# A decode step with gated attention and MLP: another layout and place for the last output weights, and a repeated TensorE block with its values behind its scores

## The chip, the cores and the metric

The kernel runs on one core of a Trainium2 chip. The metric is device time in microseconds from the start to the end of one execution; a run's time is that of its only core. Engines are named as the profile names them: PE (TensorE; PEld are its weight loads), DVE (VectorE), ACT (ScalarE), POOL (GpSimd) and SP (SyncE, which issues nearly all loads). All tensors are float32.

## The reference, cut to what matters

One token goes through an attention block over a cache of 32,768 positions and through a gated MLP, and a scalar gate mixes the two:

```python
g = _sigmoid((x * gate_w).sum(-1, keepdims=True))
q = x @ wq                                      # 32 heads of 128, D = 512
scores = einsum("bhqd,bhkd->bhqk", q, k) * Dh ** -0.5   # 8 kv heads, 4 query heads each
p = softmax(scores)
a = einsum("bhqk,bhkd->bhqd", p, v).reshape(1, 1, 4096) @ wo
b = (silu(x @ w1) * (x @ w3)) @ w2              # F = 1792
out = g * a + (1 - g) * b
```

The two caches hold 128 MB each, so nearly all of the time goes into reading them.

## The kernel before

**Tiles and buffers.** Two kv heads make a pair w, 0 to 3. The keys of a pair are read in four rounds of 8 MB, so there are 16 rounds t, 0 to 15. The values of one kv head h are read in two parts of 8 MB, v0 to v15 with number s = 2h + e. The buffer `big_a` (regions A0 and A1 of 4 MB) takes keys, `big_b` (B0 and B1) values, apart from the start, where `big_b` takes keys too. `wo_t` holds the 2 MB of wo that belong to one pair; wo0 to wo3 below are these four parts, one after the other in the same buffer.

**A round** (L453 to L476). DVE transposes the keys in 32x32 blocks, eight instructions (`scores`); PE multiplies each with the queries, laid out by ACT in `winc`; ACT copies the scores from PSUM to `sb` (`scores_out`) and PE clears the bank with a product of zeros (L244). At the end of a pair `turn` transposes the scores on PE into `turned`, and `softmax` (L378) takes the maximum and the exponentials, with DVE before and behind ACT; it leaves the probabilities in `prob` and their sums in `sums`. `weights` copies those that a value part needs to `pv`, `values_loop` multiplies them with the part on PE (64 matmul records), and `own` folds the result on DVE. Values lag behind keys by LAG = 5 rounds: PE takes v(t-5) at the head of round t.

**Order.** `Program` records every operation and derives semaphores from names of what is read and written. Each engine works strictly in the order of recording: an instruction that waits holds up everything behind it on its engine, and on SP a load that waits for its buffer holds up the loads behind it. PE's part of the 16 rounds is a hardware loop (L674 to L689), written out a second time; inside it a branch on the round's number skips values in the first rounds. Waits on other engines use counters that PE takes down (`take`).

**The end** (L568 to L655). v12 to v15 are loaded half by half: v12 and v14 through A0 and A1, v13 and v15 through `big_b`, v15 in four pieces of 4, 2, 1 and 1 MB (pieces 0 to 3; L596 to L599). v11, whose weights were made in the loop, is multiplied behind it (L579). `norm` sums `sums` over partitions and takes the reciprocal times the gate, `heads` makes the output of each head (`on`), `place` (L511) turns two pairs' outputs or one's into a row layout (`own_rows`), in which partition p holds the values of rows 8p to 8p + 7 of that pair's wo, by a DVE product, a PE product with `spot`, a DVE product with `mask` and a DVE sum. `mix_pair` then adds eight rows of wo per partition into `acc`, with eight instructions on DVE (L532). wo3 comes in another layout, one row per partition and tile (L488), so that head 6 can be mixed from `on` with four instructions on DVE and head 7 be multiplied on PE from `otp` without `place`.

**The tail.** w2 is loaded in five parts over A0 (L608). `last_head` (L555) folds the values of a head with four DVE instructions, multiplies on PE and scales into its destination. Then PE multiplies head 7's output with four tiles of wo3 (L634), DVE mixes four rows of w2 into `acc` (L635), PE takes four more rows of w2 (L637), DVE adds both (L638), and `ff_down` (L649) brings `acc` and the last six rows of w2 together; the result is copied and sent out. `idle_product` (L612) is a product whose result nobody reads; five stand between the last steps.

Of the kernel before, what the change touches and what calls it, by code (L numbers as in the profile page):

```python
# [116 lines left out]
def kernel(  # L117
# [27 lines left out]
    R = NB * DH  # L145
    NP = HKV // 2
    NH = 4 * NP
    LAG = 5
    FR = F // P
    FJ = F // 4  # L150
    assert DH == P and D == 4 * P and REP == 4 and HKV == 8 and F == FR * P and S == 4 * P * NB
# [9 lines left out]
    def sbuf(name, *shape):  # L161
        return nc.alloc_sbuf_tensor(name, [P, *shape], F32)[:]
# [12 lines left out]
    silu = tmp[:, 0].rearrange("p b d -> p (b d)")  # L175
    red = [sbuf(f"red{h}", P) for h in range(6)]
    acc = sbuf("acc", 512)
    otp = sbuf("otp", REP, 32)
    htp = sbuf("htp", FR, 32)
    turned = nc.alloc_psum_tensor("turned", [P, 2048], F32)[:]  # L180
    pf = [turned[:, 512 * f:512 * f + 512] for f in range(4)]
# [149 lines left out]
    def load_keys(t):  # L331
        b = where(t)
        for z in range(2):
            load(region(b, z), kd[t // 4, t % 4, z], ["AB"[b] + str(z)])
# [15 lines left out]
    def scores(t, z, win_op):  # L350
        kin = region(where(t), z).rearrange("p (n c j) -> p c n j", c=4, j=32)
        key = "AB"[where(t)] + str(z)
        for c in range(4):
            dst = kt[c % 2].rearrange("p (n i) -> p n i", i=32)
            k = dve(lambda c=c, d=dst: V.transpose(d, kin[:, c]), reads=[key], writes=[f"kt{c % 2}"], credit="keys")  # L355
            pe(lambda c=c: scores_part(c), reads=[f"kt{c % 2}", "winc"], writes=["s"], loop=True,
               credits=((win_op, 1), (k, 1)) if c == 0 else ((k, 1),))
# [75 lines left out]
                    )  # L433
        return ins

    def values_loop(vt, wt, loop=True):
        pe(values_all, reads=["B0", "B1", "pv", "pvpad"], writes=["o"], credits=((vt, 16), (wt, 1)), loop=loop)


    def own(s):  # L440
        h, e = divmod(s, 2)
        dve(lambda: V.tensor_tensor(
            tmp[:, e], ps_o.rearrange("p (b d) -> p b d", b=4), own_b.unsqueeze(2).to_broadcast([P, 4, P]), op=ALU.mult,
        ), reads=["o", "own_b"], writes=[f"tmp{e}"])
        if e == 1:
            dve(lambda: V.tensor_reduce(red[h], tmp.rearrange("p e b d -> p d (e b)"), axis=AX.X, op=ALU.add),  # L446
                reads=["tmp0", "tmp1"], writes=[("red", h)])
# [3 lines left out]
    vals = {}  # L451
    first = window(0, 0)
    for t in range(NH):  # L453
        scores(t, 0, first)
        second = window(t, 1)
        if t >= LAG:
            own(t - LAG)
            vals[t - LAG + 1] = (vals[t - LAG + 1], weights(t - LAG + 1))
        scores(t, 1, second)
        scores_out(t)  # L460
        if t + 1 < NH:
            load_keys(t + 1)
        if t % 4 == 3:
            turn()
        if t + 1 < NH:
            first = window(t + 1, 0)

        if t in (4, 7, 11, 15):
            softmax(t // 4 if t > 4 else 0)
        if t == LAG - 1:  # L470
            vals[0] = (vals[0], weights(0))
        if t + 1 < NH:
            if t >= LAG - 1:
                values_loop(*vals.pop(t - LAG + 1))
            if t >= LAG - 2:
                vals[t - LAG + 2] = load_values(t - LAG + 2)  # L476


    own_rows = sbuf("own_rows", 3, 8)
    each = [sbuf(f"each{i}", 2, 8, 8) for i in range(2)]  # L480

    def load_wo(w):
        src = wo[w * 8 * P:(w + 1) * 8 * P, :]
        if w < NP - 1:

            load(wo_t, src.rearrange("(p k) e -> p k e", k=8), ["wo"])
        else:
            load(wo_t, src.rearrange("(t p) e -> p t e", p=P), ["wo"])  # L488


    def norm(ws):
# [16 lines left out]
            reads=["m1"] + [("recip", h // 2) for h in hs], writes=[("on", h) for h in hs])  # L508


    def place(ws):  # L511
        i, n, w0 = ws[0] % 2, len(ws), ws[0]
        mine = each[i][:, 0:n]
        dve(lambda: V.tensor_mul(  # L514
            mine, on[:, 8 * w0:8 * w0 + 8 * n].rearrange("p (w t) -> p w t", w=n).unsqueeze(2).to_broadcast([P, n, 8, 8]),
            own_k.unsqueeze(1).unsqueeze(3).to_broadcast([P, n, 8, 8]),
        ), reads=["own_k"] + [("on", 2 * w + u) for w in ws for u in range(2)], writes=[f"each{i}"])
        pe(lambda: T.matmul(  # L518
            pm[i][:, 0:64 * n], spot.rearrange("p t x -> p (t x)"), mine.rearrange("p w k t -> p (w k t)"),
            start=True, stop=True,  # L520
        ), reads=["spot", f"each{i}"], writes=[f"m{i}"])
        dve(lambda: V.tensor_mul(
            mine, pm[i][:, 0:64 * n].rearrange("p (w k t) -> p w k t", w=n, t=8),
            mask.unsqueeze(1).unsqueeze(1).to_broadcast([P, n, 8, 8]),
        ), reads=[f"m{i}", "mask"], writes=[f"each{i}"])
        dve(lambda: V.tensor_reduce(own_rows[:, w0:w0 + n], mine, axis=AX.X, op=ALU.add),
            reads=[f"each{i}"], writes=[("own", w) for w in ws])


    def mix(o, key, ks, t=None, tkey="wo"):  # L530
        for k in ks:
            dve(lambda k=k: V.scalar_tensor_tensor(  # L532
                acc, (wo_t if t is None else t)[:, k, :], o(k), acc, op0=ALU.mult, op1=ALU.add,
            ), reads=[tkey, key, "acc"], writes=["acc"])

    def mix_pair(w):
        mix(lambda k: own_rows[:, w, k:k + 1], ("own", w), range(8))


    def values(h, e, z, vt, key, groups=range(4)):  # L540
# [14 lines left out]
    def last_head(h):  # L555
        r = red[h % 2]
        dve(lambda: V.tensor_scalar(r, ps_o[:, 0:P], own_b[:, 0:1], None, op0=ALU.mult),  # L557
            reads=["o", "own_b"], writes=[("red", h % 2)])
        for b in range(1, 4):
            dve(lambda b=b: V.scalar_tensor_tensor(  # L560
                r, ps_o[:, b * P:(b + 1) * P], own_b[:, b:b + 1], r, op0=ALU.mult, op1=ALU.add,
            ), reads=["o", "own_b", ("red", h % 2)], writes=[("red", h % 2)])
        pe(lambda: T.matmul(pm[1][:, 0:REP], r, own_q, start=True, stop=True), reads=["own_q", ("red", h % 2)], writes=["m1"])
        dst = on[:, 24:28] if h == 6 else otp[:, :, 0]
        dve(lambda: V.tensor_mul(dst, pm[1][:, 0:REP], recip[:, 4 * h:4 * h + 4]),
            reads=["m1", ("recip", 3), "otp"], writes=[("on", h)])

    def load_halves(s):  # L568
        for z in range(2):
            load(region(0, z), vd[s // 2, s % 2][:, z * R:z * R + R], [f"A{z}"])  # L570

    load_wo(0)
    load_halves(12)
    norm(range(3))
    heads(range(5))
    place((0, 1))
    mix_pair(0)
    load_wo(1)
    values_loop(*vals.pop(11), loop=False)  # L579
    load(big[1], vd[6, 1], ["B0", "B1"])  # L580
    own(11)
    norm(range(3, 4))
    heads(range(5, 6))
    mix_pair(1)
    load_wo(2)
    for z in range(2):
        values(6, 0, z, region(0, z), f"A{z}")
    load_halves(14)
    load_wo_late = lambda: load_wo(3)
    place((2,))  # L590
    mix_pair(2)
    load_wo_late()
    for z in range(2):
        values(6, 1, z, region(1, z), f"B{z}")
    last_head(6)
    cuts = (0, R, R + 4096, R + 6144, 2 * R)  # L596
    names = ("B0", "B1a", "B1b", "B1c")
    for (a, b), n in zip(zip(cuts, cuts[1:]), names):
        load(big[1][:, a:b], vd[7, 1][:, a:b], [n], over=[] if n == "B0" else ["B1"])  # L599
    mix(lambda k: on[:, 24 + k:25 + k], ("on", 6), range(4))  # L600
    for z in range(2):
        values(7, 0, z, region(0, z), f"A{z}")

# [17 lines left out]
    idle_product(512)  # L621
    idle_product(256)
    last_head(7)
    pa, pb = pf[0], pf[1]

    def ff_wide(ks, w, t, **kw):
        def go():
            for k in ks:
                j = k % 4
                ins = T.matmul(pa[32 * j:32 * j + 32, :], w(k), t(k), start=(k < 4), stop=(k >= 4))  # L630
            return ins
        pe(go, writes=["f0"], **kw)

    ff_wide(range(4), lambda k: otp[:, k, :], lambda k: wo_t[:, 4 + k, :], reads=[("on", 7), "otp", "wo"])  # L634
    mix(lambda k: htp[:, k, 0:1], "htp", range(4), w2t, ("w2", 0))  # L635
    idle_product(256)
    ff_wide(range(4, 8), lambda k: htp[:, k, :], lambda k: w2t[:, k, :], reads=["htp", ("w2", 4)])  # L637
    dve(lambda: V.tensor_add(acc, acc, pa), reads=["acc", "f0"], writes=["acc"])  # L638
    idle_product(512)

# [32 lines left out]

    with nc.Fori(0, NP, 1, engines=[PE], head_slot={PE: 0}):  # L674
        with nc.Fori(0, 4, 1, engines=[PE]):
            with T.If_cmp(half, LAG, "IS_GE"):
                take("values", 16)
                take("weights")
                values_all().then_inc(done, 1)
            with nc.Fori(0, 2, 1, engines=[PE]):  # L680
                take("windows")
                for c in range(4):
                    take("keys")
                    scores_part(c).then_inc(done, 1)
            take("scores")
            zeros().then_inc(done, 1)
            T.reg_add(half, half, 1)
        for f in range(4):
            turn_part(f).then_inc(done, 1)  # L689
# [31 lines left out]
```

## Time and profile before

| | |
|---|---|
| three runs | 697.03, 696.72, 696.99 us; median 696.99 |
| the profiled execution | 696.78 us, of which 694.8 us span |
| busy in the span | PE 405.1 us (58%), DVE 382.6 (55%), ACT 45.3 (7%), POOL 2.5 |
| mean granted TensorE clock | 0.767 |
| read from HBM | 296.23 MB, 426 GB/s over the span |

Times in all views count from the start of the span. In a timeline each line gives start, duration, engine and line, operation, what is written and read, the number of instructions taken together, and in brackets the engine's idle time before it with what ended that. The granted clock is the share of TensorE's clock pulses that the hardware let through; in this kernel it is 0.50 or 1.00 at any moment. A load's entry gives its size and the time from issue to landing; loads of one queue land in the order of their issue. A matmul in float32 shows as two records.

### The profile page before, as it was taken

Reading aid. Unit: us, or ns where it says so; the run is one execution under the profiler, and the core shown is the slowest. Engines: PE = TensorE matmul, PEld = TensorE weight load, DVE = VectorE, ACT = ScalarE, POOL = GpSimd, SP = SyncE. Lnnn points to the kernel's source line nnn. Section 1 sums busy time; section 2 is a strip of 40 time slices with the busy share of each in tenths; the row PEclk is TensorE's granted clock in tenths of the full one; section 3 lists DMA queues with packets and bytes.
Section 4 is the critical chain, followed back from the end, with each engine's and each line's share of the span. In section 5 each row is a group of like instructions: output and inputs, shape, how many; then the busy total and the mean of one; then the engine's idle time right before and its main releaser. Section 6 shows DMA issues by size and latency. Waiting matters only on the chain. (4 is left out here: it accounts for less than half of the span.)

```text
span 694.8 us, 5662 instructions
## 1 busy us (share of the span) xinstructions
PE 405.1 (58%) x2386; PEld 93.6 (13%) x2386; DVE 382.6 (55%) x274; ACT 45.3 (7%) x90; POOL 2.5 (0%) x15
## 2 busy tenths in 40 slices
PE   3626566656656656647565665647556563655447
PEld 1100011201110102101010102101010102211112
DVE  1029988796619085854629095844529095732113
ACT  0200000011100001000100001000100001000000
POOL 1000000000000000000000000000000000000000
PEclk9976888897676776867778879877886766666759
DMA  9999999999999999999999999999999999999996
GB/s 383 425 429 438 436 423 440 459 398 436 445 417 455 419 449 413 443 417 443 453 402 451 423 430 431 460 402 447 430 421 451 421 451 407 426 444 424 409 427 285
DMA packets 10421, 296.36 MB, mean 427 GB/s; under 512 B 1062, under 2 KB 1066, under 8 KB 2476
## 3 DMA queue, kind: packets, MB, share of 16 engines
q1 hardware_dynamic: 10402, 296.23, 99.2%
q8 instruction: 6, 0.10, 0.1%
q14 instruction: 3, 0.02, 0.0%
q10 hardware_dynamic: 10, 0.00, 0.0%
HBM read 296.23 MB, written 0.00 MB: 426 GB/s over the span
## 5 line engine op out<-in xcount | busy, mean ns | idle before, releaser
L355 DVE STREAM_TRANSPOSE kt<-big_a 128x2048 f32<-128x2048 f32 x112 | 250.1, 2286 | 171.1 <-DMA big_a<-in_A_k_cache_dram 165.5
L344 PE MATMUL ps<-kt,winc 128*32 128x512 f32 x1024 | 189.8, 824 | 134.4 <-PEq L671 134.4
L430 PE MATMUL ps<-big_b,pv 128*32 128x512 f32 x768 | 110.7, 741 | 59.6 <-PEq L671 59.6
L344 PEld LDWEIGHTS ps<-kt,winc 128*32 128x32 f32 x1024 | 27.1, 124 | 290.8 <-issue 290.8
L430 PEld LDWEIGHTS ps<-big_b,pv 128*32 128x32 f32 x768 | 30.0, 133 | 139.1 <-issue 139.1
L355 DVE STREAM_TRANSPOSE kt<-big_b 128x2048 f32<-128x2048 f32 x16 | 35.7, 2285 | 4.1 <-PE ps L344 2.1
L244 PE MATMUL ps<-acc 128*128 128x512 f32 x34 | 24.3, 805 | 21.8 <-PEq L671 20.3
L548 PE MATMUL ps<-big_b,probs 128*32 128x512 f32 x128 | 19.5, 771 | 22.2 <-DMA big_b<-in_A_v_cache_dram 22.2
L338 ACT COPY winc<-win 128x128 f32<-128x128 f32 x32 | 9.8, 306 | 328.0 <-PE ps L344 328.0
L532 DVE SCALAR_TENSOR_TENSOR acc<-wo_t,own_rows,acc 128x512 f32<-128x512 f32 x24 | 18.0, 752 | 23.4 <-DMA wo_t<-in_A_wo_dram 22.6
L361 ACT COPY sb<-ps 128x512 f32<-128x512 f32 x16 | 17.0, 1063 | 154.4 <-PE ps L344 154.4
L548 PE MATMUL ps<-big_a,probs 128*32 128x512 f32 x128 | 20.7, 812 | 5.8 <-DMA big_a<-in_A_v_cache_dram 5.8
L403 DVE TENSOR_REDUCE sums<-probs 128x8 f32<-128x2048 f32 x4 | 15.6, 3890 | 8.0 <-ACT probs L398 8.0
L381 DVE TENSOR_REDUCE mt<-turned 128x8 f32<-128x2048 f32 x4 | 9.1, 2282 | 17.8 <-PE turned L371 17.8
L270 PE MATMUL turned<-big_a,xp 128*32 128x512 f32 x64 | 11.9, 913 | 2.6 <-DMA big_a<-in_A_wq_dram 2.3
L307 PE MATMUL turned<-big_b,xp 128*32 128x448 f32 x64 | 7.7, 632 | 9.4 <-DMA big_b<-in_B_w_dram 9.4
L532 DVE SCALAR_TENSOR_TENSOR acc<-wo_t,on,acc 128x512 f32<-128x512 f32 x4 | 3.0, 752 | 16.4 <-DMA wo_t<-in_A_wo_dram 16.3
L244 PEld LDWEIGHTS ps<-acc 128*128 128x128 f32 x34 | 6.3, 231 | 42.2 <-issue 40.7
L446 DVE TENSOR_REDUCE red<-tmp 128x128 f32<-128x1024 f32 x6 | 11.5, 1913 | 0.2
L557 DVE TENSOR_SCALAR red<-ps,own_b 128x128 f32<-128x128 f32 x2 | 0.7, 348 | 17.8 <-PE ps L548 17.8
L518 PE MATMUL ps<-each,spot 128*128 128x128 f32 (+1 forms) x4 | 1.2, 400 | 15.0 <-DVE each L514 15.0
L398 ACT ACTIVATE probs<-turned 128x1024 f32<-128x1024 f32 x8 | 7.8, 1021 | 32.9 <-DVE turned L393 32.9
(82 smaller groups left out, 111.4 us busy)
## 6 DMA issues: line engine op xcount, KB each, us to landing
big_a<-in_A_k_cache_dram SPq DMA_DIRECT2D x28, 4096.0 KB, 28.0
big_b<-in_A_k_cache_dram SPq DMA_DIRECT2D x4, 4096.0 KB, 31.5
big_a<-in_A_v_cache_dram SPq DMA_DIRECT2D x4, 4096.0 KB, 32.6
big_a<-in_A_wq_dram SPq DMA_DIRECT2D x2, 4096.0 KB, 16.5
wo_t<-in_A_wo_dram SPq DMA_DIRECT2D x4, 2048.0 KB, 17.9
big_b<-in_B_w_dram SPq DMA_DIRECT2D x2, 3584.0 KB, 33.7
big_b<-in_A_v_cache_dram SPq DMA_DIRECT2D x1, 4096.0 KB, 27.8
big_b<-in_A_v_cache_dram SPq DMA_DIRECT2D x1, 2048.0 KB, 23.1
```

Of the source, the lines that this page charges most:

```text
L244: return T.matmul(ps_s, acc[:, 0:P], acc, start=True, stop=False, skip_group_check=True)
L270: ins = T.matmul(pf[b][32 * j:32 * j + 32, :], xp[:, c, :], t[:, o:o + REP * DH], start=(c == 0), stop=(c == NC - 1),)
L338: lambda: A.copy(winc, win[:, t // 4, :, 16 - 16 * z:48 - 16 * z]),
L344: ins = T.matmul(ps_s[32 * g:32 * g + 32, :], winc[:, c, :], kt[c % 2][:, 512 * g:512 * g + 512], start=False, stop=False, skip_group_chec ...
L355: k = dve(lambda c=c, d=dst: V.transpose(d, kin[:, c]), reads=[key], writes=[f"kt{c % 2}"], credit="keys")
L361: lambda: A.copy(sb[:, :, :, t % 4], ps_s.rearrange("p (n i) -> p n i", i=32)),
L381: dve(lambda: V.tensor_reduce(mt[:, 0:8], turned.rearrange("p (n q) -> p q n", q=8), axis=AX.X, op=ALU.max), reads=banks, writes=["mt"])
L403: dve(lambda: V.tensor_reduce(sums[:, 8 * w:8 * w + 8].rearrange("p (u q) -> p u q", u=2), probs[:, :, 0:1024].rearrange("p u (n q) -> p u ...
L430: ins = T.matmul(ps_o[32 * t:32 * t + 32, :], pv[:, o:o + 32], big[1][:, n * P:(n + 4) * P], start=((z, g) == (0, 0)), stop=((z, g) == (1, ...
L446: dve(lambda: V.tensor_reduce(red[h], tmp.rearrange("p e b d -> p d (e b)"), axis=AX.X, op=ALU.add), reads=["tmp0", "tmp1"], writes=[("red ...
L532: dve(lambda k=k: V.scalar_tensor_tensor(acc, (wo_t if t is None else t)[:, k, :], o(k), acc, op0=ALU.mult, op1=ALU.add,), reads=[tkey, ke ...
L548: ins = T.matmul(ps_o[32 * t:32 * t + 32, :], prob[u][:, o:o + 32], vt[:, n * P:(n + 4) * P], start=((e, z, g) == (0, 0, 0)), stop=((e, z, ...
```

## The change

LAG becomes 4, and PE takes v(t-4) behind the scores of round t instead of v(t-5) ahead of them; so v11 is part of the loop, ahead of the last `turn`. A softmax now stands in the round in which its first values are taken: softmax 0 stays in round 4, 1 and 2 move from rounds 7 and 11 to 8 and 12, and 3 moves from round 15 to behind the loop, after `own(11)`. All four parts of wo come in one layout, eight rows to a partition. `place` handles pairs 0 to 2 in one pass, and pair 3 in a second one behind `last_head(7)`, which writes to `otp`, now eight wide. The loads are in another order: v12, wo0, v13, wo1, v14, wo2, pieces 0 and 1 of v15, wo3, pieces 2 and 3, w2; before it was wo0, v12, wo1, v13, wo2, v14, wo3, the four pieces, w2. In the tail PE takes four rows of w2 first, then eight of wo3 (both heads of the pair), then four of w2, into one bank, and the four mixes of w2 on DVE and the four of head 6 are gone.

```diff
     NH = 4 * NP
-    LAG = 5
+    LAG = 4
     FR = F // P
...
-    otp = sbuf("otp", REP, 32)
+    otp = sbuf("otp", 8, 32)
...
-    def values_loop(vt, wt, loop=True):
-        pe(values_all, reads=["B0", "B1", "pv", "pvpad"], writes=["o"], credits=((vt, 16), (wt, 1)), loop=loop)
+    def values_loop(vt, wt):
+        pe(values_all, reads=["B0", "B1", "pv", "pvpad"], writes=["o"], credits=((vt, 16), (wt, 1)), loop=True)
...
     first = window(0, 0)
     for t in range(NH):
+        v = t - LAG
         scores(t, 0, first)
         second = window(t, 1)
-        if t >= LAG:
-            own(t - LAG)
-            vals[t - LAG + 1] = (vals[t - LAG + 1], weights(t - LAG + 1))
+        if v >= 1:
+            own(v - 1)
+            if v % 4:
+                vals[v] = (vals[v], weights(v))
         scores(t, 1, second)
         scores_out(t)
         if t + 1 < NH:
             load_keys(t + 1)
+            first = window(t + 1, 0)
+
+        if v >= 0 and v % 4 == 0:
+            softmax(v // 4)
+            vals[v] = (vals[v], weights(v))
+        if v >= 0:
+            values_loop(*vals.pop(v))
+        if v + 1 >= 0 and t + 1 < NH:
+            vals[v + 1] = load_values(v + 1)
         if t % 4 == 3:
             turn()
-        if t + 1 < NH:
-            first = window(t + 1, 0)
-
-        if t in (4, 7, 11, 15):
-            softmax(t // 4 if t > 4 else 0)
-        if t == LAG - 1:
-            vals[0] = (vals[0], weights(0))
-        if t + 1 < NH:
-            if t >= LAG - 1:
-                values_loop(*vals.pop(t - LAG + 1))
-            if t >= LAG - 2:
-                vals[t - LAG + 2] = load_values(t - LAG + 2)
 
     own_rows = sbuf("own_rows", 3, 8)
-    each = [sbuf(f"each{i}", 2, 8, 8) for i in range(2)]
...
     def load_wo(w):
-        src = wo[w * 8 * P:(w + 1) * 8 * P, :]
-        if w < NP - 1:
-
-            load(wo_t, src.rearrange("(p k) e -> p k e", k=8), ["wo"])
-        else:
-            load(wo_t, src.rearrange("(t p) e -> p t e", p=P), ["wo"])
+        load(wo_t, wo[w * 8 * P:(w + 1) * 8 * P, :].rearrange("(p k) e -> p k e", k=8), ["wo"])
...
-    def place(ws):
-        i, n, w0 = ws[0] % 2, len(ws), ws[0]
+    def place(ws, rows, i, over=()):
+        n, w0 = len(ws), ws[0]
...
-        dve(lambda: V.tensor_reduce(own_rows[:, w0:w0 + n], mine, axis=AX.X, op=ALU.add),
-            reads=[f"each{i}"], writes=[("own", w) for w in ws])
-
-
-    def mix(o, key, ks, t=None, tkey="wo"):
-        for k in ks:
+        dve(lambda: V.tensor_reduce(rows, mine, axis=AX.X, op=ALU.add),
+            reads=[f"each{i}", *over], writes=[("own", w) for w in ws])
+
+
+    def mix(w):
+        for k in range(8):
             dve(lambda k=k: V.scalar_tensor_tensor(
-                acc, (wo_t if t is None else t)[:, k, :], o(k), acc, op0=ALU.mult, op1=ALU.add,
-            ), reads=[tkey, key, "acc"], writes=["acc"])
-
-    def mix_pair(w):
-        mix(lambda k: own_rows[:, w, k:k + 1], ("own", w), range(8))
+                acc, wo_t[:, k, :], own_rows[:, w, k:k + 1], acc, op0=ALU.mult, op1=ALU.add,
+            ), reads=["wo", ("own", w), "acc"], writes=["acc"])
...
-        dst = on[:, 24:28] if h == 6 else otp[:, :, 0]
-        dve(lambda: V.tensor_mul(dst, pm[1][:, 0:REP], recip[:, 4 * h:4 * h + 4]),
-            reads=["m1", ("recip", 3), "otp"], writes=[("on", h)])
+        dve(lambda: V.tensor_mul(on[:, 4 * h:4 * h + 4], pm[1][:, 0:REP], recip[:, 4 * h:4 * h + 4]),
+            reads=["m1", ("recip", 3)], writes=[("on", h)])
...
+    load_halves(12)
     load_wo(0)
-    load_halves(12)
-    norm(range(3))
-    heads(range(5))
-    place((0, 1))
-    mix_pair(0)
-    load_wo(1)
-    values_loop(*vals.pop(11), loop=False)
     load(big[1], vd[6, 1], ["B0", "B1"])
     own(11)
-    norm(range(3, 4))
-    heads(range(5, 6))
-    mix_pair(1)
-    load_wo(2)
+    softmax(3)
+    norm(range(4))
+    heads(range(6))
+    place(range(3), own_rows, 0)
     for z in range(2):
         values(6, 0, z, region(0, z), f"A{z}")
+    mix(0)
+    load_wo(1)
     load_halves(14)
-    load_wo_late = lambda: load_wo(3)
-    place((2,))
-    mix_pair(2)
-    load_wo_late()
+    mix(1)
+    load_wo(2)
     for z in range(2):
         values(6, 1, z, region(1, z), f"B{z}")
     last_head(6)
     cuts = (0, R, R + 4096, R + 6144, 2 * R)
     names = ("B0", "B1a", "B1b", "B1c")
-    for (a, b), n in zip(zip(cuts, cuts[1:]), names):
-        load(big[1][:, a:b], vd[7, 1][:, a:b], [n], over=[] if n == "B0" else ["B1"])
-    mix(lambda k: on[:, 24 + k:25 + k], ("on", 6), range(4))
+
+    def load_piece(i):
+        a, b = cuts[i:i + 2]
+        load(big[1][:, a:b], vd[7, 1][:, a:b], [names[i]], over=["B1"] if i else [])
+
+    load_piece(0)
+    load_piece(1)
+    mix(2)
+    load_wo(3)
+    load_piece(2)
+    load_piece(3)
     for z in range(2):
         values(7, 0, z, region(0, z), f"A{z}")
 
@@ -621,20 +614,21 @@
     idle_product(512)
     idle_product(256)
     last_head(7)
+    place(range(3, 4), otp[:, :, 0].unsqueeze(1), 1, ["otp"])
     pa, pb = pf[0], pf[1]
 
-    def ff_wide(ks, w, t, **kw):
+    def wide(ws, **kw):
         def go():
-            for k in ks:
-                j = k % 4
-                ins = T.matmul(pa[32 * j:32 * j + 32, :], w(k), t(k), start=(k < 4), stop=(k >= 4))
+            for j, (w, t, first, last) in enumerate(ws):
+                r = 32 * (j % 4)
+                ins = T.matmul(pa[r:r + 32, :], w, t, start=first, stop=last)
             return ins
         pe(go, writes=["f0"], **kw)
 
-    ff_wide(range(4), lambda k: otp[:, k, :], lambda k: wo_t[:, 4 + k, :], reads=[("on", 7), "otp", "wo"])
-    mix(lambda k: htp[:, k, 0:1], "htp", range(4), w2t, ("w2", 0))
+    wide([(htp[:, k, :], w2t[:, k, :], True, False) for k in range(4)], reads=["htp", ("w2", 0)])
     idle_product(256)
-    ff_wide(range(4, 8), lambda k: htp[:, k, :], lambda k: w2t[:, k, :], reads=["htp", ("w2", 4)])
+    wide([(otp[:, k, :], wo_t[:, k, :], False, False) for k in range(8)], reads=[("own", 3), "otp", "wo"])
+    wide([(htp[:, k, :], w2t[:, k, :], False, True) for k in range(4, 8)], reads=["htp", ("w2", 4)])
     dve(lambda: V.tensor_add(acc, acc, pa), reads=["acc", "f0"], writes=["acc"])
...
         with nc.Fori(0, 4, 1, engines=[PE]):
-            with T.If_cmp(half, LAG, "IS_GE"):
-                take("values", 16)
-                take("weights")
-                values_all().then_inc(done, 1)
             with nc.Fori(0, 2, 1, engines=[PE]):
                 take("windows")
                 for c in range(4):
@@ -684,6 +674,10 @@
                     scores_part(c).then_inc(done, 1)
             take("scores")
             zeros().then_inc(done, 1)
+            with T.If_cmp(half, LAG, "IS_GE"):
+                take("values", 16)
+                take("weights")
+                values_all().then_inc(done, 1)
             T.reg_add(half, half, 1)
```

More of the change, by code (lines that the diff above doesn't have):

```diff
@@ L462 @@
             load_keys(t + 1)
+            first = window(t + 1, 0)
[6 more added lines that the diff above has]
+            vals[v + 1] = load_values(v + 1)
         if t % 4 == 3:
             turn()
-        if t + 1 < NH:
-            first = window(t + 1, 0)
-        if t in (4, 7, 11, 15):
-            softmax(t // 4 if t > 4 else 0)
-        if t == LAG - 1:
-            vals[0] = (vals[0], weights(0))
-        if t + 1 < NH:
-            if t >= LAG - 1:
-                values_loop(*vals.pop(t - LAG + 1))
-            if t >= LAG - 2:
-                vals[t - LAG + 2] = load_values(t - LAG + 2)
     own_rows = sbuf("own_rows", 3, 8)
-    each = [sbuf(f"each{i}", 2, 8, 8) for i in range(2)]
+    each = [sbuf(f"each{i}", n, 8, 8) for i, n in enumerate((3, 1))]
     def load_wo(w):
-        src = wo[w * 8 * P:(w + 1) * 8 * P, :]
-        if w < NP - 1:
-            load(wo_t, src.rearrange("(p k) e -> p k e", k=8), ["wo"])
-        else:
-            load(wo_t, src.rearrange("(t p) e -> p t e", p=P), ["wo"])
+        load(wo_t, wo[w * 8 * P:(w + 1) * 8 * P, :].rearrange("(p k) e -> p k e", k=8), ["wo"])
     def norm(ws):
```

## The prediction, made before any run of the changed kernel

> **What bounds the kernel now.** First the page's DMA rows, to see whether anything but transfers sets the length:
>
> ```profile
> DMA  9999999999999999999999999999999999999996
> q1 hardware_dynamic: 10402, 296.23, 99.2%
> ```
>
> The SP queue's packets fill 16 engines for 99.2% of 694.8 us; only the last slice is under nine tenths. The bytes stay the same, so the body can gain only by cheaper packets, and can lose only if the queue runs dry. What is left is the end, read next in the timeline of the last 25 us (start, duration, instruction, idle before):
>
> ```profile
> 672.59 9.17 PE L548 MATMUL ps<-big_b,probs 128*32 128x512 f32 x56 [9.72 <-DMA big_b<-in_A_v_cache_dram]
> ...
> 682.75 1.07 PE L548 MATMUL ps<-big_b,probs 128*32 128x512 f32 x8
> 683.88 0.35 DVE L557 TENSOR_SCALAR red<-ps,own_b 128x128 f32<-128x128 f32 x1 [17.84 <-PE ps L548]
> ...
> 685.45 0.39 PE L563 MATMUL ps<-own_q,red 128*128 128x4 f32 x2
> 685.87 0.17 DVE L565 TENSOR_TENSOR otp<-ps,recip 128x4 f32<-128x4 f32 x1 [0.48 <-PE ps L563]
> 685.95 3.10 DVE L532 SCALAR_TENSOR_TENSOR acc<-big_a,htp,acc 128x512 f32<-128x512 f32 x4
> 686.09 1.06 PE L630 MATMUL turned<-wo_t,otp 128*32 128x512 f32 x8 [0.26 <-DVE otp L565]
> 687.08 0.70 PE L613 MATMUL ps<-sb,ones 128*128 128x256 f32 x2
> 687.71 1.06 PE L630 MATMUL turned<-big_a,htp 128*32 128x512 f32 x8
> 689.15 0.69 DVE L638 TENSOR_TENSOR acc<-acc,turned 128x512 f32<-128x512 f32 x1
> ```
>
> Piece 0 of v15 lands at 672.55 (issued 644.78, 27.8 to landing), and from there TensorE works almost without a break until the last values end at E = 682.75 + 1.07 = 683.82. Then comes a serial tail: `last_head`, then four w2 mixes on DVE to 689.05, which end later than TensorE's products (688.77); the addition starts at 689.15 = E + 5.33. The last w2 piece lands at 691.1 (658.48 + 32.6), where the last products run (690.14 to 691.63). DMA and tail end together.
>
> **The change, part by part.**
>
> *Main loop.* TensorE's order is nearly the old one (values of t-4 behind the scores of t were values of t-5 ahead of the next scores); only `turn` goes behind values, and softmaxes 1 and 2 come a round later. DVE's idle time after a round's transposes hides them. In that round the transposes end at 295.10 + 8.95 = 304.05. A softmax gives its probabilities 9.0 after its start (269.87; second ACTIVATE 277.8 + 1.02), and `weights` takes 0.61: 313.6, where those values started at 313.03. So they end 0.6 late, and the next value load goes out at 322.6 instead of 322.00, while the keys ahead of it in the queue land some 10 us later (second key load 305.3 + 28). Cost 0; without that cover 0.6 each.
>
> *The twelfth values* go into the loop: v11 lands at 584.5 (554.54 + 30), so they run from 584.6 to 594.2 (9.59 before, from 594.96 on), and v13's transfer goes out at 594.3, not 604.63. `own(11)` (0.69 + 1.87) and softmax 3 (580.41 to 593.10, 12.7) follow to 609.6. The norm now waits for the sums; norm, heads and `place` took 2.7 (593.01 to 595.67); with 0.4 for the norm's product and wider tiles I take 3.4: 613.0. The mix of wo0 (6.26) ends at 619.3, and wo1 goes out, with v14's halves behind it on SP.
>
> *Landings.* A load lands when all ahead of it has: 9.71 per 4 MB half, 19.4 for v13 (613.7 to 633.1), 4.88 per wo, 2.45 per 1 MB piece. In the new order, from 584.5 on: v12 594.2 and 603.9, wo0 608.8, v13 628.2, wo1 633.1, v14 642.8 and 652.5, wo2 657.4, pieces 0 and 1 667.1 and 672.0, wo3 676.9, pieces 2 and 3 679.4 and 681.9. Does the queue have work at every issue? wo1 at 619.3 against 628.2, wo3 at 657.4 + 6.26 = 663.7 against 672.0, with pieces 2, 3 and w2 behind it on SP. On DVE `last_head(6)` waits behind the mix of wo1 until 639.4, but the values behind it wait for v14 until 642.8 anyway. Margins of 8 us: the later mixes cost 0.
>
> *wo3's rows.* In the old layout it took 5.34 (657.50 to 662.84), the others 4.88 (633.09 to 637.97): the new one gains 0.46, and piece 3 moves from 682.4 (halfway between piece 2 at 679.9 and the first w2 piece at 684.9) to 681.9. The Trainium skill ("DMA: Bandwidth & Descriptors", Specifications) puts line rate at 512 B and more; by that 2 KB rows lose nothing, and the time below would be 0.46 higher. The rows here differ, and they decide.
>
> *Values of v15.* Pieces 0 and 1 come 5.4 us sooner. Their 48 products' records go at four per 0.86 at half clock and per 0.43 at full (weight loads of 0.20 + 0.66 at 673.45, 0.12 + 0.31 at 679.01): from 667.2, with full clock after 3.4 to 6.8 us, they end at 674.0 to 675.7, and TensorE idles until piece 2 at 679.4. What such a gap does to the clock stands in a table of stretches (length; busy us of PE, PEld, DVE, ACT, POOL; clock; DMA share, GB/s):
>
> ```profile
> 651.29:654.70 3.41, 1.82 (x20) 0.29 (x12) 0.00 (x0) 0.00 (x0) 0.00 (x0) 1.00 0.96 414
> 654.70:658.11 3.41, 0.57 (x8) 0.27 (x12) 0.00 (x0) 0.00 (x0) 0.00 (x0) 1.00 0.93 353
> 658.11:661.53 3.42, 3.42 (x24) 0.87 (x19) 0.00 (x0) 0.00 (x0) 0.00 (x0) 0.50 1.16 447
> ...
> 671.77:675.18 3.41, 2.59 (x16) 0.63 (x20) 0.00 (x0) 0.00 (x0) 0.00 (x0) 0.50 0.97 411
> 675.18:678.59 3.41, 3.41 (x24) 0.79 (x20) 0.00 (x0) 0.00 (x0) 0.00 (x0) 0.50 0.99 413
> 678.59:682.00 3.41, 3.41 (x33) 1.02 (x26) 0.00 (x0) 0.00 (x0) 0.00 (x0) 1.00 1.02 423
> ```
>
> A stretch with 0.57 busy is followed by half clock; only a full one (3.41) gives full clock back, 2.59 did not. The Trainium skill ("TensorE: Matmul & The Clock Gate", Part 1: The HAM clock gate) says the same of one idle window of about 3.4 us; the rows agree.
>
> At full clock piece 3 ends at 681.95 + 1.07 = 683.05. At half clock eight records take 1.94 (299.74, L344) and the 512-wide idle product ahead of piece 3 about 1.9 (2.03 at 306.52, L244): piece 2 from 679.4 to 681.25, idle product to 683.15, piece 3 to 685.1 if half clock holds. It ends after one full stretch, between 682.8 and 686.2, so E is 684.0 to 685.1. I take 684.5, 0.7 later than before.
>
> *The tail from E.* `last_head` stays: its result starts at E + 2.05. New is `place` for the last pair:
>
> ```profile
> 619.93 0.22 DVE L514 TENSOR_TENSOR each<-on,own_k 128x64 f32<-128x64 f32 x1
> 620.67 0.22 DVE L522 TENSOR_TENSOR each<-ps,mask 128x64 f32<-128x64 f32 x1 [0.53 <-PE ps L518]
> 620.93 0.22 DVE L526 TENSOR_REDUCE own_rows<-each 128x8 f32<-128x64 f32 x1
> ```
>
> `each` follows at +0.21 (593.68 to 593.89) and its product 0.27 later (620.20), so TensorE takes it at E + 2.53; `otp` is ready 1.22 after `each`, at E + 3.5. Behind that product, which holds TensorE some 0.35, stand in TensorE's order: w2 rows 0 to 3 (1.00, 686.09 to 687.08), an idle product (0.63, to 687.71), eight wo products instead of four (1.00, and 0.86 for eight more records), w2 rows 4 to 7 (1.06). That is E + 2.88, 3.88, 4.51, 6.37, 7.43: the addition starts at E + 7.45, and `otp` is not what it waits for. DVE's 3.10 of w2 mixes go, worth the 0.3 by which they ended after TensorE. The tail grows by 2.1. What follows the addition is unchanged, and w2 (last piece now 690.7) no longer holds it.
>
> **Sum.** Addition at 684.5 + 7.45 = 691.95 against 689.15: +2.8. The profiled execution took 696.78 (694.8 and 1.98 around it), 0.21 under the median of the runs, 696.99. 696.78 + 2.8 = **699.6 us**.
>
> **Rivals.**
> *Full clock throughout:* E 683.05, addition 690.5, +1.35, 698.1. For it: 1.82 busy of 3.41 kept full clock, so a gap cut by a stretch's border may pass. Against: the gap is 3.7 to 5.4 us, longer than a stretch. 0.15.
> *Half clock into the tail:* E 685.1; the idle products of 512 and 256 take about 3.0 instead of 1.6 and hold `last_head`'s product back by 1.4: addition 693.95, +4.8, 701.6. For it: 2.59 of 3.41 stayed at half. Against: from 679.4 on TensorE is busy. 0.14.
> *Not slower:* TensorE takes the first w2 group and the idle product (1.63) while DVE folds; the tail is 5.8, the addition comes at 683.05 + 5.8 = 688.85, −0.3, 696.5. It decides once the tail is under 6.1 at full clock. For it: the first w2 piece lands at 684.4. Against: both stand behind `place`'s product in program order. 0.07.
> *The queue runs dry:* each us by which wo1 or wo3 goes out past 628.2 or 672.0 is lost; with the chain to wo1 12 us longer than summed, 3 us on top of the forecast, 702.6. Against: the margins. 0.04.
>
> **How the numbers follow.** Forecast 0.60, its own range 698.8 to 700.4. The range for 8 in 10 reaches into both clock cases: 697.9 to 701.3. A measurement here tells about 0.2% (1.4 us) from no change. Slower by more: forecast, half clock, dry queue and a small part of the full-clock case, 0.79; within: the rest of that case and most of not-slower, 0.19; faster by more 0.02, since the DMA bound leaves no such gain.
>
> **What would show it.** Right: DMA full to 685; wo1 issued near 619, wo3 near 664; a PE gap of some 4 us before piece 2 and half clock near 680; L557 starting 0.2 to 1.3 later than 683.88; the addition about 7.4 after E. Wrong: DMA slices under nine tenths earlier, values of v15 without a gap, or w2's first products ahead of `place`'s.

## The result, and the profile after

The changed kernel takes 699.52 us (median of six runs, 699.08 to 699.89) where the kernel before takes 696.88; the ratio is 1.0037, with a 95% interval of 1.0024 to 1.005. The fastest run of the changed kernel (699.08) is slower than the slowest before (697.03), so 0.4% stands clear of the noise here. The span of its six runs is 697.3 to 698.1, median 697.8, against 694.8 in the profiled execution before. The prediction was 699.6 us, slower. One run of experiment 8 below took 1735.13 us, for an unknown reason, and is in none of the comparisons.

The page's DMA rows of the changed kernel, to be read as before:

```profile
DMA  9999999999999999999999999999999999999994
q1 hardware_dynamic: 9506, 296.23, 98.6%
```

The queue is full in every slice but the last, for the same bytes; it is only the last slice that holds less. There are 896 packets fewer (10402 before): wo3 came in 1,024 rows of 2 KB and now comes in 128 of 16 KB. The difference is therefore at the end. The timeline of the last 32 us (start, duration, instruction, idle before):

```profile
667.09 7.17 PE L540 MATMUL ps<-big_b,probs 128*32 128x512 f32 x48 [9.27 <-DMA big_b<-in_A_v_cache_dram]
679.35 1.94 PE L540 MATMUL ps<-big_b,probs 128*32 128x512 f32 x8 [5.09 <-DMA big_b<-in_A_v_cache_dram]
...
681.21 2.07 PE L606 MATMUL ps<-sb,ones 128*128 128x512 f32 x2
683.22 1.65 PE L540 MATMUL ps<-big_b,probs 128*32 128x512 f32 x8
...
684.94 0.35 DVE L549 TENSOR_SCALAR red<-ps,own_b 128x128 f32<-128x128 f32 x1 [21.32 <-PE ps L540]
...
686.93 0.16 DVE L556 TENSOR_TENSOR on<-ps,recip 128x4 f32<-128x4 f32 x1 [0.48 <-PE ps L555]
...
687.41 0.43 PE L513 MATMUL ps<-each,spot 128*128 128x64 f32 x2 [0.51 <-DVE each L509]
687.77 1.06 PE L624 MATMUL turned<-big_a,htp 128*32 128x512 f32 x8
...
688.77 0.70 PE L606 MATMUL ps<-sb,ones 128*128 128x256 f32 x2
689.40 1.92 PE L624 MATMUL turned<-wo_t,otp 128*32 128x512 f32 x16
691.14 1.04 PE L624 MATMUL turned<-big_a,htp 128*32 128x512 f32 x8
692.11 1.12 PE L606 MATMUL ps<-sb,ones 128*128 128x512 f32 x2
692.25 0.69 DVE L632 TENSOR_TENSOR acc<-acc,turned 128x512 f32<-128x512 f32 x1 [3.89 <-PE turned L624]
693.16 0.43 PE L639 MATMUL turned<-acc,ones 128*32 128x128 f32 x8
```

Pieces 0 and 1 of v15 are multiplied by 674.26, then TensorE waits 5.09 us for piece 2. Eight records take 1.94 there, and the idle product 2.07, where before the same took 1.07 and 1.12. The values end at 683.22 + 1.65 = 684.87, 1.05 later than before, and the addition starts 7.38 later, at 692.25, 3.10 after the old 689.15. The table of stretches shows the clock (length; busy us of PE, PEld, DVE, ACT, POOL; clock; DMA share, GB/s):

```profile
670.79:674.20 3.41, 3.41 (x32) 0.73 (x24) 0.00 (x0) 0.00 (x0) 0.00 (x0) 1.00 1.00 428
674.20:677.62 3.42, 0.06 (x4) 0.00 (x0) 0.00 (x0) 0.00 (x0) 0.00 (x0) 1.00 0.96 398
677.62:681.03 3.41, 1.68 (x8) 0.20 (x8) 0.00 (x0) 0.00 (x0) 0.00 (x0) 0.50 1.01 423
681.03:684.45 3.42, 3.42 (x14) 0.71 (x10) 0.00 (x0) 0.00 (x0) 0.00 (x0) 0.50 1.01 420
684.45:687.86 3.41, 2.74 (x16) 1.36 (x16) 1.79 (x6) 0.00 (x0) 0.00 (x0) 1.00 1.00 410
```

A stretch with 0.06 us of work takes full clock away, and it comes back only after the full stretch that ends at 684.45, when all but the last 0.42 us of the values is done. The last w2 piece lands at 690.5 and no longer holds anything.

### The profile page after: what moved, and what is told of

The parts are those of the page before. It is cut to its first block, busy times and chain, and to the rows that moved or that the text cites. A ratio compares the mean times of both kernels' runs of the same rounds, so it can differ in the third digit from the quotient of the medians.

```text
span 698.1 us, 5677 instructions
## 1 busy us (share of the span) xinstructions
PE 402.4 (58%) x2400; PEld 94.3 (14%) x2400; DVE 376.1 (54%) x263; ACT 45.3 (6%) x90; POOL 2.6 (0%) x15
## 5 line engine op out<-in xcount | busy, mean ns | idle before, releaser
L344 PE MATMUL ps<-kt,winc 128*32 128x512 f32 x1024 | 183.0, 795 | 132.1 <-PEq L665 131.9
L244 PE MATMUL ps<-acc 128*128 128x512 f32 x34 | 22.2, 740 | 21.8 <-PEq L665 20.2
L540 PE MATMUL ps<-big_a,probs 128*32 128x512 f32 x128 | 19.2, 759 | 5.5 <-DMA big_a<-in_A_v_cache_dram 5.5
L442 DVE TENSOR_TENSOR tmp<-ps,own_b 128x512 f32<-128x512 f32 x12 | 7.9, 656 | 19.8 <-PE ps L430 19.8
L307 PE MATMUL turned<-big_b,xp 128*32 128x448 f32 x64 | 10.5, 826 | 8.2 <-DMA big_b<-in_B_w_dram 8.2
L393 DVE TENSOR_TENSOR turned<-turned,top 128x2048 f32<-128x2048 f32 x4 | 9.2, 2300 | 0.1
L540 PEld LDWEIGHTS ps<-big_b,probs 128*32 128x32 f32 x128 | 4.4, 137 | 35.9 <-DMA big_b<-in_A_v_cache_dram 23.8
```

Of the source, the lines that this page charges most:

```text
L244: return T.matmul(ps_s, acc[:, 0:P], acc, start=True, stop=False, skip_group_check=True)
L307: ins = T.matmul(pf[2 + z][32 * j:32 * j + 32, 0:FJ], xp[:, c, :], t[:, o:o + FJ], start=(c == 0), stop=(c == NC - 1),)
L344: ins = T.matmul(ps_s[32 * g:32 * g + 32, :], winc[:, c, :], kt[c % 2][:, 512 * g:512 * g + 512], start=False, stop=False, skip_group_chec ...
L540: ins = T.matmul(ps_o[32 * t:32 * t + 32, :], prob[u][:, o:o + 32], vt[:, n * P:(n + 4) * P], start=((e, z, g) == (0, 0, 0)), stop=((e, z, ...
```

## The experiments

Times are medians; each is compared with runs of the kernel before on the same chip, 696.73 us for the first four and 696.97 for the last four. The span of every run is known too, to 0.1 us; its median before is 694.8 on the first chip and 694.9 on the second. "Around the span" means a run's time less its span.

**1. Idle products in the gap.**

```diff
+        if n == "B1b":
+            for _ in range(4):
+                idle_product(512)
```

> The changed kernel with four idle products of 512 columns in TensorE's gap between pieces 1 and 2 of v15. My theory (half clock after the gap costs 1.1 to 1.8 us, the longer tail the rest): the clock stays full, the last values end at about 683.1 instead of 684.9, the addition starts at about 690.5 instead of 692.3, and the time is 697.8 to 698.1. Rival (the whole loss is the work of the longer tail, the clock beside it costs nothing): 699.5, as without them.

It took 698.42, ratio 1.0027 (1.0017 to 1.0036), instead of 699.52. Its timeline:

```profile
674.37 3.70 PE L606 MATMUL ps<-sb,ones 128*128 128x512 f32 x8
...
679.47 1.07 PE L540 MATMUL ps<-big_b,probs 128*32 128x512 f32 x8 [1.40 <-DMA big_b<-in_A_v_cache_dram]
...
681.95 1.06 PE L540 MATMUL ps<-big_b,probs 128*32 128x512 f32 x8 [0.36 <-DMA big_b<-in_A_v_cache_dram]
...
690.39 0.69 DVE L635 TENSOR_TENSOR acc<-acc,turned 128x512 f32<-128x512 f32 x1 [3.88 <-PE turned L627]
```

and two of its stretches:

```profile
677.88:681.29 3.41, 2.01 (x11) 0.46 (x10) 0.00 (x0) 0.00 (x0) 0.00 (x0) 1.00 1.01 420
681.29:684.70 3.41, 2.90 (x14) 0.88 (x13) 1.40 (x4) 0.00 (x0) 0.00 (x0) 1.00 1.01 419
```

With work whose result nobody reads in the gap, pieces 2 and 3 run at 1.07 and 1.06, and the values end at 683.01: landing sets it, not the clock. The addition starts at 690.39, as the full-clock rival of the prediction had it (690.5). The median is 0.3 above the expected band, since the runs spread from 697.85 to 699.63. The spread lies outside the span: all ten spans lie between 696.1 and 696.4, and the time around the span goes from 1.75 to 3.33. By the spans, filling the gap gains 1.6 (697.8 less 696.2).

**2. The old end on the new order of loads.** wo3 in its old layout, head 6 on DVE, head 7 without `place`, four w2 rows on DVE:

```diff
...
-    place(range(3, 4), otp[:, :, 0].unsqueeze(1), 1, ["otp"])
...
-    wide([(htp[:, k, :], w2t[:, k, :], True, False) for k in range(4)], reads=["htp", ("w2", 0)])
+    wide([(otp[:, k, :], wo_t[:, 4 + k, :], True, False) for k in range(4)], reads=[("on", 7), "otp", "wo"])
+    mix_rows(lambda k: htp[:, k, 0:1], "htp", range(4), w2t, ("w2", 0))
     idle_product(256)
-    wide([(otp[:, k, :], wo_t[:, k, :], False, False) for k in range(8)], reads=[("own", 3), "otp", "wo"])
```

> The changed kernel with the old end: wo3 in the old layout, head 6 mixed on DVE, head 7 without place, four rows of w2 on DVE; loop, softmaxes and order of loads stay changed. My theory: the tail from the end of the values is again 5.3 us, but the gap and its half clock stay and wo3 takes 0.46 longer, so the values end near 685.3, the addition starts near 690.6 and the time is about 698.3. Rival (the loss comes from the loop, the later softmaxes or the order of loads): about 699.5. Rival (all of the loss is the tail): 696.9.

It took 698.24, ratio 1.002 (1.0011 to 1.0029). Values and addition in its timeline:

```profile
683.86 1.28 PE L544 MATMUL ps<-big_b,probs 128*32 128x512 f32 x8
...
690.50 0.69 DVE L643 TENSOR_TENSOR acc<-acc,turned 128x512 f32<-128x512 f32 x1
```

The tail is 690.50 − 685.14 = 5.36 again, and the late values stay. Neither the tail nor the gap alone is the loss.

**3. Both: old end and filled gap** (the edits of 1 and 2).

> Old end and four idle products in the gap together; what is left of the change is the loop, the later softmaxes and mixes, and the order of loads. My theory (these cost nothing): values end at 683.5, the last piece of w2 lands at 691.1 as before and sets the end, 696.7 to 697.0, the same as before. Rival (they cost something that the tail hides): above 697.3.

It took 696.69, ratio 1.0002 (0.9993 to 1.0011): no difference. What is left of the change in it, the loop, the later softmaxes and mixes and the new order of loads, costs nothing that can be measured. Its runs fall into two groups, six at 696.41 to 696.69 (the median is the slowest of them) and five at 697.34 to 697.53. The difference is in the span, 694.6 to 694.9 in the lower group, as before the change, and 695.6 or 695.7 in the upper. The profiled one (697.42) is of the upper group; its piece 2 and its stretches show what happened there:

```profile
679.90 1.34 PE L544 MATMUL ps<-big_b,probs 128*32 128x512 f32 x8 [2.23 <-DMA big_b<-in_A_v_cache_dram]
...
673.73:677.15 3.42, 3.42 (x12) 1.44 (x8) 0.00 (x0) 0.00 (x0) 0.00 (x0) 1.00 1.07 410
677.15:680.56 3.41, 1.18 (x10) 0.16 (x8) 3.01 (x4) 0.00 (x0) 0.00 (x0) 1.00 1.00 418
680.56:683.97 3.41, 3.41 (x10) 0.70 (x10) 0.00 (x0) 0.00 (x0) 0.00 (x0) 0.50 1.02 423
```

Here piece 2 comes 0.4 later than in experiment 1, the gap left behind the four idle products is 2.23 us, and it falls into one stretch: 1.18 busy, and half clock for the next. That the lower group kept full clock is an inference; only one execution has a profile.

**4. wo3's rows alone, on the kernel before.**

```diff
-        if w < NP - 1:
-            load(wo_t, src.rearrange("(p k) e -> p k e", k=8), ["wo"])
-        else:
-            load(wo_t, src.rearrange("(t p) e -> p t e", p=P), ["wo"])
+        load(wo_t, src.rearrange("(p k) e -> p k e", k=8), ["wo"])
```

> The kernel before with one edit, wo3 in rows of eight to a partition; the products with wo3 then pair outputs with other rows of wo than the reference does, and the amount of work is the same. My theory: wo3 takes 4.9 instead of 5.3 us in the queue, everything behind it comes 0.4 to 0.5 us sooner, 696.4 to 696.5. Rival (rows of 2 KB lose nothing): 696.9.

It took 696.17, 0.56 less. The ratio of 0.9992 has an interval of 0.9983 to 1.0001, which just includes no change, but its slowest run (696.49) is below the fastest of the kernel before (696.51). The spans say the same (694.2 against 694.8), and in the profile wo3 lands 4.9 behind the last half of v14 (657.3 to 662.2) instead of 5.34. The rows' gain is there, and near the 0.4 to 0.5 expected.

**5. The first w2 group ahead of `place`.** In TensorE's order:

```diff
-    idle_product(512)
-    idle_product(256)
-    last_head(7)
-    place(range(3, 4), otp[:, :, 0].unsqueeze(1), 1, ["otp"])
...
     wide([(htp[:, k, :], w2t[:, k, :], True, False) for k in range(4)], reads=["htp", ("w2", 0)])
     idle_product(256)
+    last_head(7)
+    place(range(3, 4), otp[:, :, 0].unsqueeze(1), 1, ["otp"])
+    idle_product(256)
```

> The changed kernel with the first w2 group and an idle product ahead of last_head's product instead of behind place's, in the place of the two idle products there. My theory (in the tail the addition waits for TensorE's list behind place's product, not for otp): the eight wo products start when otp is ready, 3.5 us after the end of the values instead of 4.5, the addition about 6.4 after it instead of 7.4, and the time is 698.4 to 698.6. Rival (DVE's place is the bound of the tail): 699.5, no change.

It took 698.86, ratio 1.0025 (1.0014 to 1.0036). Its timeline:

```profile
683.29 1.89 PE L540 MATMUL ps<-big_b,probs 128*32 128x512 f32 x8
685.00 1.04 PE L620 MATMUL turned<-big_a,htp 128*32 128x512 f32 x8
...
688.45 0.22 DVE L521 TENSOR_REDUCE otp<-each 128x8 f32<-128x64 f32 x1
688.72 1.92 PE L620 MATMUL turned<-wo_t,otp 128*32 128x512 f32 x16
...
691.57 0.69 DVE L631 TENSOR_TENSOR acc<-acc,turned 128x512 f32<-128x512 f32 x1 [2.90 <-PE turned L620]
```

The wo products now start as soon as `otp` is written (688.67), and the tail is 691.57 − 685.18 = 6.39, against 7.38. The full microsecond is gained where the theory put it. The median fell by 0.75 against the kernel before (+1.89 instead of +2.64), 0.3 less than expected; in the profiled execution half clock lasted to 685.0, so the values ended 0.3 later.

**6. wo3 ahead of pieces 0 and 1.**

```diff
-    load_piece(0)
-    load_piece(1)
     mix(2)
     load_wo(3)
+    load_piece(0)
+    load_piece(1)
```

> The changed kernel with wo3 issued ahead of pieces 0 and 1 of v15, so that these wait on SP for the mix of wo2 as well. My theory (the mixes come so late that the queue has work only because these pieces stand ahead): the queue is empty from 657.4 until the mix ends at 663.7, everything behind comes some 6.3 us later, pieces 0 and 1 no longer come ahead of wo3 so that TensorE has no gap, values end near 691.5, and the time is 705.5 to 707. Rival (the order of these loads does not matter): 699.5.

It took 708.5, ratio 1.0165 (1.0151 to 1.0178), 1.5 above the band expected. Its stretches around the mix of wo2:

```profile
655.00:657.50 2.50, 2.50 (x24) 0.69 (x16) 0.00 (x0) 0.00 (x0) 0.00 (x0) 0.72 0.17 72
657.54:663.85 6.31, 0.52 (x8) 0.00 (x0) 6.01 (x8) 0.00 (x0) 0.00 (x0) 0.95 0.00 0
663.85:666.70 2.85, 0.00 (x0) 0.00 (x0) 0.00 (x0) 0.00 (x0) 0.00 (x0) 0.50 0.70 172
666.70:671.60 4.90, 0.00 (x0) 0.00 (x0) 0.00 (x0) 0.00 (x0) 0.00 (x0) 0.50 1.02 435
```

and the landing of wo3 and the last values:

```profile
wo_t<-in_A_wo_dram SPq DMA_DIRECT2D x1, 2048.0 KB, 7.7
...
692.52 1.06 PE L540 MATMUL ps<-big_b,probs 128*32 128x512 f32 x8 [1.07 <-DMA big_b<-in_A_v_cache_dram]
```

The transfers stand still for the 6.31 us of DVE's mix, as summed, and the theory is right that the order of loads hides it. What the expectation left out is the restart: wo3, issued at 663.85, lands 7.7 us later, where 4.88 is its time in a full queue. The empty queue cost its idle time and some 2.8 us more, 9.1 in all by the time piece 0 lands (681.2, where a full queue gives 657.5 + 4.88 + 9.71 = 672.1). Piece 3 lands 1.4 later still than its bytes ask; why stays open. This kernel has no gap ahead of piece 2 and runs its last values at full clock (1.06), so the 9.0 us by which it is slower than the changed kernel hides the clock's share; against experiment 8, which keeps full clock too, it is 10.4.

**7. Five idle products in the gap, and a shorter tail.**

```diff
-    wide([(htp[:, k, :], w2t[:, k, :], True, False) for k in range(4)], reads=["htp", ("w2", 0)])
-    idle_product(256)
...
-    wide([(htp[:, k, :], w2t[:, k, :], False, True) for k in range(4, 8)], reads=["htp", ("w2", 4)])
...
+    ff_down([(htp[:, k, :], w2t[:, k, :], k == 0, False) for k in range(4)], reads=["htp", ("w2", 0)])
+    wide([(otp[:, k, :], wo_t[:, k, :], k < 4, k >= 4) for k in range(8)], reads=[("own", 3), "otp", "wo"])
+    ff_down([(htp[:, k, :], w2t[:, k, :], False, False) for k in range(4, 8)], reads=["htp", ("w2", 4)])
     dve(lambda: V.tensor_add(acc, acc, pa), reads=["acc", "f0"], writes=["acc"])
+    ff_down([(ones[:, 0:32], acc, False, False)], reads=["ones", "acc"])
```

> The changed kernel with five idle products in the gap, and with w2 rows 0 to 7 taken in the narrow products of ff_down, rows 0 to 3 while place's result is made and rows 4 to 7 during the addition, and without the last two idle products. My theory: values end at 683.1, the addition starts 5.8 us later at 688.9, TensorE is done at about 691.3 where it was 691.6 before the change, 696.3 to 696.6. Rival (place's detour alone keeps the tail longer than the old one): 697 or more.

It took 696.29, ratio 0.9991 (0.9983 to 1.0): 0.68 less than the kernel before, with an interval that just touches no change (0.4 by the spans, 694.5 against 694.9), and 3.2 less than the changed kernel. Its timeline:

```profile
685.73 1.08 PE L635 MATMUL turned<-big_a,htp 128*32 128x128 f32 x32
...
686.63 1.90 PE L627 MATMUL turned<-wo_t,otp 128*32 128x512 f32 x16
688.35 1.06 PE L635 MATMUL turned<-big_a,htp 128*32 128x128 f32 x32
688.60 0.69 DVE L642 TENSOR_TENSOR acc<-acc,turned 128x512 f32<-128x512 f32 x1 [2.28 <-PE turned L627]
689.34 0.43 PE L635 MATMUL turned<-acc,ones 128*32 128x128 f32 x8
689.58 1.49 PE L635 MATMUL turned<-big_a,htp 128*32 128x128 f32 x48
```

Four w2 rows fit behind `place`'s product, four more run beside the addition, and the last products end at 691.07, 0.6 after the last piece of w2 lands (690.5 in the changed kernel, whose order of loads this is). So little remains of the tail beyond the transfers.

**8. Five idle products without the shorter tail** (the edit of 1 with `range(5)`).

> As e1_fill, with five idle products instead of four, so that the gap ahead of piece 2 is under one us where it was 1.4. My theory (e1_fill's runs from 697.85 to 699.63 are a coin flip of the clock over what gap remains): nearly all runs lie between 697.7 and 698.3. Rival (the spread has another cause): runs up to 699.6 as with four.

It took 698.10, ratio 1.0018 (1.0009 to 1.0027). Eight runs lie between 697.94 and 698.12, which is the band expected, and three between 698.70 and 699.18. One of these three (699.11) is the profiled one, and it had full clock from 671.44 on and a span of only 696.3. So the theory of a coin flip of the clock is refuted: all eleven spans lie between 696.1 and 696.6, and what makes the later runs late is mostly the time around the span, 2.8 us in two of the three, where the changed kernel has 1.7 to 1.8. The spans of experiment 1 say the same. What makes that time longer stays open.

## Why the prediction was right

*Nothing in the body.* Right. Issues and landings came as listed: wo3 out at 663.65 (663.7), piece 2 landed at 679.3 (679.4). The largest miss is wo1, out at 621.1 instead of 619.3, since the products of `heads` took 2.70 at half clock; the queue had work until 628.1, so it cost nothing. Experiment 3 shows that the loop, the softmaxes and the late mixes cost nothing; experiment 6 shows what hides the mixes, and that the price without that cover is about 10 us for the mix of wo2 alone.

*wo3's rows, 0.46.* Right: the packets became fewer, and experiment 4 measured 0.56. The rule of the Trainium skill ("DMA: Bandwidth & Descriptors", Specifications), by which rows of 512 B and more run at line rate, would have left the time as it was; the measurement favours the trace's rows.

*The clock.* Right in mechanism and nearly in size. The gap was 5.09 us, full clock went, and the values ended at 684.87, inside 684.0 to 685.1 and 0.4 above the value taken. (The sum's 683.05 for the values at full clock should read 683.02, which changes nothing.) What the gap costs is read best from the spans: 697.8 with it, 696.2 and 696.3 with it filled (experiments 1 and 8), so 1.5 to 1.6, as the sum had between its rival at full clock and its forecast. The differences of the medians, 0.95 (2.64 less 1.69) and 1.5 (2.64 less 1.13), carry the time around the span with them. On the old end the two groups of experiment 3 lie 0.9 apart. A stretch need not be idle to lose the clock: 0.06, 1.18 and 0.57 busy in a stretch lost it, 1.82 and 2.01 kept it. The Trainium skill ("TensorE: Matmul & The Clock Gate", Part 1) has an idle window of about 3.4 us that takes the clock away. The nearly idle stretch of the changed kernel (0.06 busy) agrees; the 1.18 busy of experiment 3 was not idle, and there the measurement goes beyond what the Trainium skill says.

*The tail.* Right: 7.38 against 7.45 summed. What bounds it is TensorE's list behind `place`'s product, as the sum said and experiment 5 shows, and not `otp`. Undoing the tail gives 5.36.

*The rivals.* Full clock throughout came only with the filled gap. Half clock into the tail did not come in the profiled execution, where full clock is back at 684.45. Not slower needs both cures, a filled gap and either the old tail (experiment 3) or a shorter one (experiment 7); moving the first w2 group alone, as that rival had it, gives 1.0 us of the tail's 2.1. That rival's tail of 5.8 was mis-summed: it let the wo products start at E + 2.88, ahead of `otp` at E + 3.5, and with `otp` it comes to 6.4; experiment 5 measured 6.39. The dry queue comes only with another order of loads, and its price was too low: the rival took the idle time alone, and experiment 6 shows 2.8 us of restart on top.

*What the sum left out* is small. The idle product of 512 columns that stands beside the addition begins at 692.11 and still holds TensorE when the addition ends at 692.94; so the first narrow product starts at 693.16, 0.91 after the addition's start, where it was 0.75. Before, the addition came 0.44 after that idle product's start instead of 0.14, and it was in nobody's way. That 0.16 and the 0.4 of the values, less 0.07 of the tail, are why the profiled span grew by 3.3 instead of 2.8. Over the six runs the span is 3.0 above 694.8, and the time grew by 2.64. That the sum meets the median within 0.1 is in part luck: it took 697.6 for the span and 1.98 around it, and the six runs have a median span of 697.8 and only 1.7 to 1.8 around it.

## What to carry to other kernels

Where transfers fill the whole run, an early landing is worth nothing by itself: here it only opened a gap in TensorE's work, and the clock lost in it came out of the few microseconds that no transfer hides. Read the serial tail in program order on its busiest engine, not as a chain of data alone; work that needs nothing belongs in the waits ahead of the late operand, not behind its product. And before a load is put behind a wait, see what the queue still holds at that moment: an empty queue costs its idle time and the restart.

## What the runs showed of the hardware beside that

A queue that had run dry took about 2.8 us more than the transfer until the next load had landed (7.7 instead of 4.88 for 2 MB, experiment 6, one case). Read in short stretches of that trace, no byte moves from 656.5 to 664.6: the queue is empty 1.0 before the mix can start at 657.5, and the first bytes of wo3 move some 0.75 behind its issue at 663.85. Until 667.0 they move at 131 to 328 GB/s, and at 410 and more after that.

A load in rows of 2 KB was also followed by a long hold of the issuing engine. SP's timeline in the kernel before, behind wo3 in its old layout:

```profile
644.36 0.38 SPq L191 DMA_DIRECT2D wo_t<-in_A_wo_dram  x1
644.78 10.68 SPq L191 DMA_DIRECT2D big_b<-in_A_v_cache_dram  x3
```

and in experiment 4, with eight rows to a partition:

```profile
644.22 0.33 SPq L191 DMA_DIRECT2D wo_t<-in_A_wo_dram  x1
644.59 1.85 SPq L191 DMA_DIRECT2D big_b<-in_A_v_cache_dram  x4
```

Issuing three loads behind the 1,024 rows took 10.68 us, four loads behind 128 rows 1.85. It cost nothing here because the queue was full, but a load that was urgent would have waited. Such holds are not peculiar to 2 KB rows: in experiment 4 the five loads of w2 that follow took 12.94 us to issue, and in the changed kernel the two halves of v12 took 10.62. A limit on what may be queued ahead would fit all three; no run tests it.
